# First batch of an attention-and-experts kernel: q and k of all four pairs of heads resident, row maxima one by one between tiles, the first pair's in two PSUM tiles

## Chip, cores and metric

The kernel runs on one core of a Trainium2 chip. The metric is device time in microseconds (us) of one execution. The engines are TensorE (PE, with its weight loads as PEld), VectorE (DVE), ScalarE (ACT), GpSimd (POOL) and SyncE (SP), which issues most DMAs. Each engine runs its own instructions in order and waits on semaphores for the others.

## Reference

```python
scores = matmul(q, k.transpose(0, 1, 3, 2)) / sqrt(64)      # q, k, v: (4 batches, 8 heads, 576, 64)
thresh = max(scores, axis=-1) - tau
scores = where(scores >= thresh, scores, -1e9)
attn   = exp(scores - max(scores)); attn /= attn.sum(-1) + 1e-9
x = (attn @ v).transpose(0, 2, 1, 3).reshape(2304, 512)
h = x @ w_in                                                  # first expert, 512 -> 2048 -> 512
x = ((a0 + a1*h + a2*h**2 + a3*h**3) / (1 + |b0|*|h| + |b1|*h**2 + 1e-6)) @ w_out
h = x @ w2_in                                                 # second expert, same sizes
y = where(h >= 1, h, where(h <= -1, 0, (h + 1)**2 / 4)) @ w2_out
```

The weights of both experts are stored as 64-bit floats; the kernel turns them into 16-bit pieces itself.

## The kernel before

The program has two stages. In the first, up to about 235 us, the attention of batch 0 runs alone (`first_attention`), while the sixteen weight halves of the first expert are loaded and converted beside it. In the second, the tokens go through the two experts in steps, a batch at a time; the attention of batches 1 to 3 and the sixteen halves of the second expert's weights (`w2`) are laid beside these steps.

Batch 0 is worked through in four pairs of heads, 0 to 3. For a pair, `prep_pair` loads q and k (tile `rqk`), scales and casts them on ScalarE (L203), takes the remainder on GpSimd (L207), transposes both by one DMA of 18 blocks of 128 x 128 into `qkT` (L339), and copies the two halves of k crosswise into `kT2` (L341, L342). Then `row_max` finds the row maxima. It makes eleven score tiles `sm` (eight of 512 columns, one of eight small pieces `t`, `r` and `rt`): two dots each on TensorE (L506, L507) and one reduction on VectorE (L510), all through one PSUM tile of tag `ph0`. The maxima are cut in three 16-bit pieces (`pcs`, L537, L539), turned into rows by small products `pmr` in the PSUM tile `aux` (L545; this tile also serves the products `pmmw`, `pg` and `pmmqke` of the weights and of the scales), and ScalarE copies them into `mrow` (L546). Only then can the nine tiles of the pair begin. A tile's transposed scores `st` are six products, of which every third subtracts the row maxima (L562 to L564); ScalarE takes the exponential (L566), VectorE applies the threshold (L567), and TensorE sums over v (L576). At the end of a pair ScalarE copies the sums out (L583, L584), and VectorE divides (L590 to L592) and writes the two 16-bit parts of the result `xT` (L597).

The weight halves go through VectorE in three passes (L223 to L225, `rw` to `wt`), ScalarE (L212, L241, L203) and GpSimd (L207).

`row_max` is a generator: in the tiles 0, 2 and 4 of a pair the program takes one step of the next pair's maxima, and after tile 5 it prepares the pair after that one.

```python
rows = row_max(pr + 1, *ahead[0][1:]) if ahead else iter(())
...
    if n % 9 in (0, 2, 4):
        mrow = next(rows, None)
    if n % 9 == 5 and pr + 2 < NP:
        ahead.append(prep_pair(0, pr + 2, False))
```

Written order is not yet the engines' order. Each of the `N_FIRST` steps of `first_attention` and each half of the weights gets a priority (`at(...)`), and a scheduler places every engine's instructions by priority and by its own estimate of when they are ready. The engines then run that order.

Of the kernel before, what the change touches and what calls it, by code (L numbers as in the profile page):

```python
# [9 lines left out]
F16 = mybir.dt.float16  # L10
# [29 lines left out]
def tile_attention_moe_moe2(  # L40
# [20 lines left out]
    P = 128  # L61
# [250 lines left out]
    def prep_pair(b, pr, on_vector=True):  # L312
# [39 lines left out]
    def scores(s, t, ab, qkT, kT2):  # L352
# [6 lines left out]
        k1 = qkT[:, C:, :].rearrange("p c s -> p (c s)")  # L359
        k2 = kT2.rearrange("p c s -> p (c s)")  # L360
        for rows, c, cols, keys in parts:
            at = 0
            for k0, n in keys:
                while n:
                    w = min(n, 512 - at % 512)
                    T.matmul(s[rows, at : at + w], qkT[:, c, cols], k1[:, k0 : k0 + w], start=True, stop=False)  # L366
                    T.matmul(s[rows, at : at + w], qkT[:, c, cols], k2[:, k0 : k0 + w], start=False, stop=True)  # L367
                    at, k0, n = at + w, k0 + w, n - w
# [127 lines left out]
    def row_max(pr, qkT, kT2):  # L496
        k1 = qkT[:, C:, :].rearrange("p c s -> p (c s)")
        k2 = kT2.rearrange("p c s -> p (c s)")
        mx = sp.tile([P, 18], F32, name=f"mx0_{pr}", tag="c2", bufs=3)

        def bank(name):
            return ps_1.tile([P, 512], F32, name=f"sm{pr}_{name}", tag="ph0")

        def dots(dst, c, cols, k0):
            n = dst.shape[-1]
            T.matmul(dst, qkT[:, c, cols], k1[:, k0 : k0 + n], start=True, stop=False)  # L506
            T.matmul(dst, qkT[:, c, cols], k2[:, k0 : k0 + n], start=False, stop=True)  # L507

        def most(n, src, m=1):
            V.tensor_reduce(mx[:, n : n + m], src, axis=AX.X, op=ALU.max)  # L510

        halves = [slice(i * ST, (i + 1) * ST) for i in range(2)]
        for ab in range(2):
# [4 lines left out]
            yield  # L518
# [12 lines left out]
        most(3 * NT + 1, s)  # L531
        n = 2 * NT + 1
# [7 lines left out]
        mrow = ap.tile([P, 2 * S], F16, name=f"mrow{pr}", tag="hl", bufs=N_ROW)  # L540
        G.memset(mrow, 0.0)
# [5 lines left out]
        yield mrow  # L547

    def transposed(pr, ab, t, data, n):

        con, qkT, kT2, mrow = data
# [3 lines left out]
        q1 = qkT[:, 0:C, :].rearrange("p c s -> p (c s)")  # L555
# [46 lines left out]
    def first_attention():  # L602

        ahead = [prep_pair(0, 0, False)]
        yield
        vv = first_v()
        yield
        xT[0] = [xp.tile([P, 2 * KT, TB], F16, name=f"xT0_{j}", tag="xT", bufs=NB) for j in range(NB)]
        ahead.append(prep_pair(0, 1, False))
        yield  # L610
        for mrow in row_max(0, *ahead[0][1:]):
            yield
        n = 0
        for pr in range(NP):
            con, qkT, kT2 = ahead.pop(0)
            data = con, qkT, kT2, mrow
            rows = row_max(pr + 1, *ahead[0][1:]) if ahead else iter(())
# [3 lines left out]
            for ab, t in [(0, t) for t in range(NT + 1)] + [(1, t) for t in range(NT)]:  # L621
# [24 lines left out]
    N_FIRST = 7 + 9 * NP  # L646
# [288 lines left out]
```

## Time and profile before

| what | us |
|---|---|
| three runs | 1308.18, 1313.86, 1312.43 (median 1312.43) |
| profiled execution | 1311.16, of which its span 1309.2 |
| TensorE busy | 1096.2 (84% of the span) |
| VectorE busy | 1022.1 (78%) |
| ScalarE busy | 823.1 (63%) |
| GpSimd busy | 504.7 (39%) |
| granted TensorE clock, mean over the span | 0.929 of full speed |

Busy time is time in which an engine executes; the span runs from the first instruction to the last. The stages of a program can have different limits, so the shares of the whole span are the first thing to look at and not the last.

### The profile page before, as it was taken

The page shows a single profiled execution, that of the slowest core. Times are in us where ns is not written, and L with a number is a line of the kernel's source. Part 1 is how long each engine was busy: PE and PEld are TensorE (multiplying, and loading weights), DVE is VectorE, ACT ScalarE, POOL GpSimd, SP SyncE. Part 2 cuts the span into 40 slices and gives each one's busy share as a digit, 9 for nine tenths or more (in the row PEclk, how much of TensorE's full clock was granted, in tenths as well). Part 3 has the DMA queues.
Part 4 walks back from the last instruction along what each step waited for, and adds up shares of the span by engine and source line. Part 5 has one row for each costly group of instructions (what it writes and reads, how often), then busy time and mean ns, then how long its engine had stood idle before and what let it go on. Part 6 is the DMA issues. An engine that isn't in the chain of part 4 may idle for free.

```text
span 1309.2 us, 31145 instructions
## 1 busy us (share of the span) xinstructions
PE 1096.2 (84%) x12354; PEld 977.9 (75%) x12354; DVE 1022.1 (78%) x2403; ACT 823.1 (63%) x1477; POOL 504.7 (39%) x678
## 2 busy tenths in 40 slices
PE   2686667678862799989988999999798999999998
PEld 1253334577751688889878899898688988999997
DVE  6676566989987987768999776799997767897431
ACT  3466446677745667767677577677775767676332
POOL 3123214444543564542146455421473554122221
PEclk9997768798985799989989999999999999999999
DMA  7625333533477765692359664911685559105100
GB/s 204 197 97 162 121 129 133 200 119 105 150 262 217 167 126 109 122 222 86 87 134 226 127 114 101 258 62 46 174 202 112 103 100 267 46 2 210 50 14 26
DMA packets 220274, 176.35 MB, mean 135 GB/s; under 512 B 181984, under 2 KB 193248, under 8 KB 211936
## 3 DMA queue, kind: packets, MB, share of 16 engines
q1 hardware_dynamic: 220128, 174.36, 50.0%
q8 instruction: 97, 1.59, 0.5%
q14 instruction: 49, 0.40, 0.1%
HBM read 106.83 MB, written 21.50 MB: 98 GB/s over the span
## 4 chain that ended last, share of the span: by engine, by line
PE 36%; DVE 15%; DMA 10%; issue 3%; POOL 3%; ACT 2%; SPq 1%; DVEq 0%; ACTq 0%; POOLq 0%
PE acc L834 15%; PE ph L820 15%; DMA eT<-hl 6%; PE pv L400 2%; DVE e L374 2%; POOL hl L385 2%; DMA qkT<-qk 2%; DVE sc L412 1%; DVE t L713 1%; DVE t L712 1%; PE s L367 1%; PE s L366 1%; DVE qk L210 1%; DMA rqk<-in_k_dram 1%; DVE t L714 1%
## 5 line engine op out<-in xcount | busy, mean ns | idle before, releaser
L834 PE MATMUL acc<-gg,wc 128*128 128x192 f16 x4608 | 431.9, 248 | 26.0 <-POOL gg L207 16.7
L820 PEld LDWEIGHTS <-wc 128*128 128x128 f16 x4608 | 393.4, 100 | 30.0 <-DVE t L709 20.2
L834 PEld LDWEIGHTS <-wc 128*128 128x128 f16 x4608 | 386.0, 99 | 29.1 <-issue 27.3
L207 POOL TENSOR_TENSOR gg<-t,gg 128x384 f16<-128x384 f32 x192 | 192.3, 1003 | 413.8 <-ACT gg L203 353.5
L820 PE MATMUL ph<-xT,wc 128*128 128x192 f16 x2304 | 221.4, 254 | 19.1 <-DVE t L709 15.1
L820 PE MATMUL ph<-yT,wc 128*128 128x192 f16 x2304 | 218.8, 249 | 1.6 <-DVE t L709 1.1
L385 POOL TENSOR_TENSOR hl<-e,hl 128x256 f16<-128x256 f32 x216 | 155.8, 741 | 0.0
L203 ACT CAST gg<-t 128x384 f16<-128x384 f32 x192 | 97.2, 508 | 69.4 <-DVE t L767 36.5
L374 DVE SCALAR_TENSOR_TENSOR e<-sc,nt,e 128x576 f32<-128x576 f32 x108 | 95.7, 886 | 32.3 <-ACT e L373 31.6
L766 DVE SCALAR_TENSOR_TENSOR t<-t,c 128x384 f32<-128x384 f32 x96 | 63.8, 664 | 69.9 <-ACT t L765 69.8
L383 POOL TENSOR_TENSOR hl<-e,hl 128x64 f16<-128x64 f32 x108 | 40.6, 376 | 165.2 <-ACT hl L382 162.4
L373 ACT ACTIVATE e<-sc,nt,con 128x576 f32<-128x576 f32 x108 | 93.5, 866 | 8.7 <-POOL hl L385 1.4
L382 ACT CAST hl<-e 128x576 f16<-128x576 f32 x108 | 72.3, 669 | 41.0 <-DVE e L374 39.0
L705 ACT ACTIVATE t<-ph,sc 128x384 f32<-128x384 f32 x96 | 55.4, 577 | 63.0 <-PE ph L820 62.9
L400 PE MATMUL pv<-v,eT 128*128 128x65 f16 (+3 forms) x1680 | 71.7, 196 | 25.3 <-DMA eT<-hl 25.2
L412 DVE TENSOR_SCALAR_CACHE_REDUCE sc<-s 128x576 f32<-128x576 f32 x108 | 80.8, 749 | 14.9 <-PE s L367 14.3
L765 ACT ACTIVATE t<-ph,c 128x384 f32<-128x384 f32 x96 | 63.8, 666 | 44.3 <-PE ph L820 43.7
L400 PEld LDWEIGHTS <-eT 128*128 128x128 f16 (+1 forms) x1680 | 64.3, 102 | 34.5 <-DMA eT<-hl 32.1
L207 POOL TENSOR_TENSOR wc<-wt,wc 128x256 f16<-128x256 f32 x64 | 47.7, 778 | 94.2 <-ACT wc L203 94.2
L710 ACT ACTIVATE t<-t,lc 128x384 f32<-128x384 f32 x96 | 67.9, 708 | 23.4 <-DVE t L707 22.9
L366 PE MATMUL s<-qkT 128*128 128x512 f16 (+1 forms) x240 | 65.0, 294 | 15.9 <-DVE sc L412 11.2
L712 DVE SCALAR_TENSOR_TENSOR t<-t,ka,t 128x384 f32<-128x384 f32 x96 | 65.8, 686 | 14.7 <-ACT t L711 14.0
(216 smaller groups left out, 1857.4 us busy)
## 6 DMA issues: line engine op xcount, KB each, us to landing
wc<-scratch SPq DMA_DIRECT2D x56, 1024.0 KB, 5.7
rw<-in_moe_w_in_dram SPq DMA_DIRECT2D x16, 1024.0 KB, 5.4
rw<-in_moe_w_out_dram SPq DMA_DIRECT2D x16, 1024.0 KB, 5.0
scratch<-wc SPq DMA_DIRECT2D x8, 1024.0 KB, 3.8
scratch<-wh SPq DMA_DIRECT2D x16, 512.0 KB, 3.0
kT<-qkT SPq DMA_DIRECT2D x32, 144.0 KB, 2.4
rqk<-in_q_dram SPq DMA_DIRECT2D x16, 256.0 KB, 3.1
rqk<-in_k_dram SPq DMA_DIRECT2D x16, 256.0 KB, 3.0
```

The costliest lines, as they stand in the source:

```text
L203: A.copy(hi, src)
L207: G.tensor_tensor(lo[:, p], src[:, p], hi[:, p], op=ALU.subtract)
L366: T.matmul(s[rows, at : at + w], qkT[:, c, cols], k1[:, k0 : k0 + w], start=True, stop=False)
L373: A.activation(e, s, AF.Exp, bias=nb, scale=con[:, 0:1])
L374: V.scalar_tensor_tensor(e, s, th, e, op0=ALU.is_ge, op1=ALU.mult)
L382: A.copy(hi, e)
L385: G.tensor_tensor(lo_w[:, p], e[:, whole][:, p], hi[:, whole][:, p], op=ALU.subtract)
L400: T.matmul(pv[rows, 0:w], eT[:, c, cols], vv[:, h * NT + x if x < NT else H * NT + h, at : at + w], start=(n == 0), stop=(n == len(blocks) ...
L412: V.tensor_scalar(s, banks[:, 0:S], 1.0, -LARGEST, op0=ALU.mult, op1=ALU.max, accum_out=mx)
L712: V.scalar_tensor_tensor(s, s, ka[:, 0:1], r, op0=ALU.add, op1=ALU.mult)
L820: last = T.matmul(ph[:, f, :], w[:, wx, kt, f * P : (f + 1) * P], rhs, start=(n == 0), stop=(n == 3 * KT - 1))
L834: T.matmul(dst, w[:, wx, f, d * P : (d + 1) * P], gg[:, gx, f, :], start=(i == 0 and f == 0 and n == 0 and d % 2 == 0), stop=(i == NCH - 1 ...
```

## The change

Pairs 2 and 3 get buffers of their own for q and k: three tiles each (`qT`, `kT`, `kT2`), in buffers of tags `eT` and `hl` that only the later batches used. They are filled by two transposes of nine blocks in place of one of eighteen. So all four pairs are prepared ahead of the first tile in written order. The two `mrow` tiles are fixed and cleared once. `row_max` gives way after each of its tiles (eleven steps in place of three); in each of a pair's first four tiles the program takes two steps of the next pair's maxima, in the others one. The first pair's maxima use two PSUM tiles (`acc` and `s`) in turn. `N_FIRST`, over which the priorities are spread, goes from 43 to 53.

```diff
-        qkT = ap.tile([P, 2 * C, P], F16, name=f"qkT{b}_{pr}", tag="qkT")
-        Q.dma_start_transpose(out=qkT, in_=qk.rearrange("p x c d -> p (x c d)"))
-        kT2 = ap.tile([P, C, P], F16, name=f"kT2{b}_{pr}", tag="kT2")
-        Q.dma_start(kT2[0:D], qkT[D : 2 * D, C : 2 * C, :])
-        Q.dma_start(kT2[D : 2 * D], qkT[0:D, C : 2 * C, :])
-        return con, qkT, kT2
+        if b > 0 or pr < 2:
+            qkT = ap.tile([P, 2 * C, P], F16, name=f"qkT{b}_{pr}", tag="qkT")
+            Q.dma_start_transpose(out=qkT, in_=qk.rearrange("p x c d -> p (x c d)"))
+            qT, kT = qkT[:, 0:C], qkT[:, C : 2 * C]
+            kT2 = ap.tile([P, C, P], F16, name=f"kT2{b}_{pr}", tag="kT2")
+        else:
+            qT, kT, kT2 = (ap.tile([P, C, P], F16, name=f"{x}{b}_{pr}", tag="eT" if pr == 2 else "hl", bufs=N_ROW)
+                           for x in ("qT", "kT", "kT2"))
+            for x, t in enumerate((qT, kT)):
+                Q.dma_start_transpose(out=t, in_=qk[:, x].rearrange("p c d -> p (c d)"))
+        Q.dma_start(kT2[0:D], kT[D : 2 * D])
+        Q.dma_start(kT2[D : 2 * D], kT[0:D])
+        return con, qT, kT, kT2
...
-    def row_max(pr, qkT, kT2):
+    def row_max(pr, qT, kT, kT2, mrow):
...
+        count = [0]
...
         def bank(name):
-            return ps_1.tile([P, 512], F32, name=f"sm{pr}_{name}", tag="ph0")
+            if pr > 0:
+                return ps_1.tile([P, 512], F32, name=f"sm{pr}_{name}", tag="ph0")
+            count[0] += 1
+            return ps_2.tile([P, 1024], F32, name=f"sm{pr}_{name}", tag="acc" if count[0] % 2 else "s")[:, 0:512]
...
-            yield
+                yield
...
-        mrow = ap.tile([P, 2 * S], F16, name=f"mrow{pr}", tag="hl", bufs=N_ROW)
-        G.memset(mrow, 0.0)
...
-        yield mrow
+        yield
...
-        ahead = [prep_pair(0, 0, False)]
+        pairs = [prep_pair(0, 0, False)]
...
+        mrows = [xp.tile([P, 1152], F16, name="mrow0", tag="yT", bufs=NB), mp.tile([P, 1152], F16, name="mrow1", tag="yo", bufs=1)]
+        for t in mrows:
+            G.memset(t, 0.0)
         yield
-        ahead.append(prep_pair(0, 1, False))
+        pairs.append(prep_pair(0, 1, False))
         yield
-        for mrow in row_max(0, *ahead[0][1:]):
+        for _ in row_max(0, *pairs[0][1:], mrows[0]):
+            yield
+        for pr in range(2, NP):
+            pairs.append(prep_pair(0, pr, False))
             yield
...
-                if n % 9 in (0, 2, 4):
-                    mrow = next(rows, None)
-                if n % 9 == 5 and pr + 2 < NP:
-                    ahead.append(prep_pair(0, pr + 2, False))
+                for _ in range(2 if n % 9 < 4 else 1):
+                    next(rows, None)
...
-    N_FIRST = 7 + 9 * NP
+    N_FIRST = 17 + 9 * NP
```

The change moves instructions on three engines. In the names below, `sm2_13` is a score tile of pair 2's maxima, `et1_0_0` the exponentials of pair 1's first tile, `st1_0_0` its scores, and the last number of a name is the buffer's serial number. Lines of the changed program lie 7 to 14 further down: the reduction is L521, the threshold L578, the passes over weights stay L223 to L225.

On VectorE, pair 2's maxima stand before the change between pair 1's last tile and pair 2's first:

```order
L510 TENSOR_REDUCE mx0_2_802<-sm2_13_887 128x1
L510 TENSOR_REDUCE mx0_2_802<-sm2_t_944 128x4 x2
L510 TENSOR_REDUCE mx0_2_802<-sm2_r_963 128x1
L510 TENSOR_REDUCE mx0_2_802<-sm2_rt_969 128x1
L534 TENSOR_TENSOR mx0_2_802<-mx0_2_802 128x9
L537 TENSOR_SCALAR pcs2_976<-mx0_2_802 128x9
L539 SCALAR_TENSOR_TENSOR mx0_2_802<-pcs2_976,mx0_2_802 128x9
...
L537 TENSOR_SCALAR pcs2_976<-mx0_2_802 128x9
L567 SCALAR_TENSOR_TENSOR et2_0_0_1153<-st2_0_0_1146,con0_2_691,et2_0_0_1153 128x576
```

With the change they stand between pair 0's result and pair 1's first tile:

```order
L608 SCALAR_TENSOR_TENSOR xT0_2_260<-x0_0_576,v0_s_254,xT0_2_260 128x192
L521 TENSOR_REDUCE mx0_2_898<-sm2_00_899 128x1
L521 TENSOR_REDUCE mx0_2_898<-sm2_01_903 128x1
...
L521 TENSOR_REDUCE mx0_2_898<-sm2_r_1077 128x1
L224 SCALAR_TENSOR_TENSOR wt0_4_0_929<-rw0_4_0_927,wt0_4_0_929 128x1024
L521 TENSOR_REDUCE mx0_2_898<-sm2_rt_1083 128x1
L225 SCALAR_TENSOR_TENSOR wt0_4_0_929<-rw0_4_0_927,wt0_4_0_929 128x1024
L223 TENSOR_SCALAR wt0_4_1_1038<-rw0_4_1_1036 128x1024
L547 TENSOR_TENSOR mx0_2_898<-mx0_2_898 128x9
L521 TENSOR_REDUCE mx0_3_1215<-sm3_00_1216 128x1
L578 SCALAR_TENSOR_TENSOR et1_0_0_893<-st1_0_0_886,con0_1_286,et1_0_0_893 128x576
```

The whole block of eleven moved up by one pair; pair 3's maxima (`sm3`), which stood behind pair 2's tiles, follow among pair 1's tiles.

On TensorE, the products that turn pair 1's maxima into rows (`pmr1`) stand before the change right behind the first products of pair 1's first tile, in the last tiles of pair 0:

```order
L576 MATMUL pv1_0_1_669<-et0_1_2_728,v32_222 128x288
L562 MATMUL st1_0_0_790<-qkT0_1_293 128x288
L563 MATMUL st1_0_0_790<-qkT0_1_293,kT20_1_295 128x288
L545 LDWEIGHTS pcs1_597
L545 MATMUL pmr1_0_605<-fixed_90,pcs1_597 3x128
...
L545 MATMUL pmr1_4_611<-fixed_90,pcs1_597 3x128
...
L564 MATMUL st1_0_0_790<-mrow1_603,fixed_90 128x288
```

With the change, ten of pair 2's eleven score tiles come in front of them:

```order
L573 MATMUL st1_0_1_907<-qkT0_1_297 128x288
L574 MATMUL st1_0_1_907<-qkT0_1_297,kT20_1_299 128x288
L517 MATMUL sm2_00_899<-kT0_2_531,qT0_2_530 128x512
L518 MATMUL sm2_00_899<-kT20_2_532,qT0_2_530 128x512
...
L517 MATMUL sm2_r_1077<-kT0_2_531,qT0_2_530 64x512
...
L556 MATMUL pmr1_0_802<-fixed_90,pcs1_796 3x128
...
L556 MATMUL pmr1_4_808<-fixed_90,pcs1_796 3x128
...
L575 MATMUL st1_0_0_886<-mrow1_262,fixed_90 128x288
```

So pair 1's row products moved behind pair 2's maxima, and with them the end of pair 1's first scores.

On SyncE's queue, a transpose of pair 1 stood behind two loads of weights, and pair 2's was one DMA:

```order
L236 DMA rw0_2_0_620<-in_moe_w_in_dram 128x4x512
L236 DMA rw0_2_1_733<-in_moe_w_out_dram 128x2x1024
L339 DMA_TRANSPOSE qkT0_1_293<-qk0_1_269 128x18x128
L316 DMA rqk0_2_670<-in_q_dram 128x2x256
...
L236 DMA rw0_4_1_1175<-in_moe_w_out_dram 128x2x1024
L339 DMA_TRANSPOSE qkT0_2_702<-qk0_2_678 128x18x128
L316 DMA rqk0_3_1017<-in_q_dram 128x2x256
L319 DMA rqk0_3_1017<-in_q_dram 64x64
L341 DMA kT20_2_704<-qkT0_2_702 64x1152
L342 DMA kT20_2_704<-qkT0_2_702 64x1152
```

With the change one of the two loads stands behind pair 1's transpose, and pair 2's transposes are two:

```order
L236 DMA rw0_1_1_386<-in_moe_w_out_dram 128x2x1024
L236 DMA rw0_2_0_466<-in_moe_w_in_dram 128x4x512
L340 DMA_TRANSPOSE qkT0_1_297<-qk0_1_273 128x18x128
L316 DMA rqk0_2_498<-in_q_dram 128x2x256
...
L236 DMA rw0_4_1_1036<-in_moe_w_out_dram 128x2x1024
L347 DMA_TRANSPOSE qT0_2_530<-qk0_2_506 128x9x128
L347 DMA_TRANSPOSE kT0_2_531<-qk0_2_506 128x9x128
L316 DMA rqk0_3_537<-in_q_dram 128x2x256
L319 DMA rqk0_3_537<-in_q_dram 64x64
L348 DMA kT20_2_532<-kT0_2_531 64x1152
L349 DMA kT20_2_532<-kT0_2_531 64x1152
```

Pair 2's transposes keep their place behind the weight loads up to `rw0_4_1`.

## Rows read from the trace of the kernel before

**Rows 1.** Busy time, share of the span and instructions of each engine
```profile
PE 1096.2 (84%) x12354; PEld 977.9 (75%) x12354; DVE 1022.1 (78%) x2403; ACT 823.1 (63%) x1477; POOL 504.7 (39%) x678
```

**Rows 2.** Windows cut at ScalarE's first and last exponentials of each pair
```profile
core 0: us, PE busy (x) PEld busy (x) DVE busy (x) ACT busy (x) POOL busy (x), PEclk, DMA share, GB/s
59.87:80.42 20.55, 19.83 (x125) 12.30 (x124) 15.74 (x32) 13.33 (x22) 4.11 (x7) 1.00 0.19 70
80.42:88.02 7.60, 4.94 (x29) 2.85 (x29) 5.55 (x8) 4.49 (x12) 1.98 (x3) 1.00 0.43 160
88.02:111.80 23.78, 19.70 (x102) 13.12 (x102) 16.12 (x38) 18.21 (x31) 4.19 (x6) 0.93 0.23 82
111.80:147.02 35.22, 18.69 (x77) 7.90 (x76) 22.75 (x39) 13.48 (x27) 11.20 (x13) 0.53 0.60 191
147.02:168.53 21.51, 18.52 (x104) 12.50 (x104) 14.64 (x33) 13.59 (x22) 5.08 (x6) 0.98 0.39 100
168.53:194.21 25.68, 14.86 (x83) 7.95 (x81) 16.82 (x32) 11.84 (x22) 5.72 (x9) 0.63 0.40 139
194.21:214.81 20.60, 18.50 (x98) 12.41 (x97) 14.51 (x29) 14.45 (x23) 6.64 (x8) 0.88 0.28 103
214.81:236.09 21.28, 10.88 (x56) 8.61 (x57) 15.18 (x49) 14.99 (x27) 6.67 (x9) 0.61 0.55 196
236.09:262.00 25.91, 15.89 (x140) 14.76 (x139) 25.01 (x45) 15.32 (x26) 16.10 (x14) 0.79 0.51 180
```

**Rows 3.** VectorE's timeline, pair 2's maxima: start, duration, line, operation, [idle <-releaser]
```profile
130.29 0.69 DVE L510 TENSOR_REDUCE mx<-sm 128x1 f32<-128x512 f32 x1 [1.10 <-PE sm L507]
132.09 0.69 DVE L510 TENSOR_REDUCE mx<-sm 128x1 f32<-128x512 f32 x1 [1.10 <-PE sm L507]
```

**Rows 4.** The same timeline, pair 3's maxima
```profile
173.50 0.69 DVE L510 TENSOR_REDUCE mx<-sm 128x1 f32<-128x512 f32 x1 [0.68 <-PE sm L507]
174.87 0.69 DVE L510 TENSOR_REDUCE mx<-sm 128x1 f32<-128x512 f32 x1 [0.68 <-PE sm L507]
```

**Rows 5.** Timelines of VectorE and ScalarE, last piece to first exponential of pair 2
```profile
142.81 0.17 DVE L537 TENSOR_SCALAR pcs<-mx 128x9 f16<-128x9 f32 x1
147.02 1.37 ACT L566 ACTIVATE et<-st,con 128x576 f32<-128x576 f32 x2
```

**Rows 6.** Timelines of ScalarE and TensorE, pair 2's cast and first dot
```profile
109.72 1.23 ACT L203 CAST qk<-rqk 128x576 f16<-128x576 f32 x2
120.02 0.61 PE L507 MATMUL sm<-kT,qkT 128*128 128x512 f16 x1 [0.52 <-DMA kT<-qkT]
```

**Rows 7.** View of tile eT, and DMA list (median us, issue to landing)
```profile
L387 SPq DMA_TRANSPOSE eT<-hl x108: 1242/1298/4039, 430.0 to 1105.0; - x108
...
eT<-hl SPq DMA_TRANSPOSE x108, 3.5
...
qkT<-qk SPq DMA_TRANSPOSE x16, 4.0
```

**Rows 8.** Timelines of SyncE's queue and TensorE, pair 1's transpose and first dot
```profile
41.30 5.62 SPq L339 DMA_TRANSPOSE qkT<-qk  x1
52.00 0.59 PE L506 MATMUL sm<-qkT 128*128 128x512 f16 x1 [0.32 <-DVE mx L510]
```

**Rows 9.** Groups by line and shape, 0 to 300 us (busy, mean ns)
```profile
L224 DVE SCALAR_TENSOR_TENSOR wt<-rw,wt 128x1024 int32<-128x1024 int32 x23 | 29.5, 1282 | 0.2
...
L223 DVE TENSOR_SCALAR wt<-rw 128x1024 int32<-128x1024 int32 x24 | 18.9, 786 | 6.8 <-POOL wc L207 3.3 <-DMA rw<-in_moe_w_out_dram 3.1 <-DMA rw<-in_moe_w_in_dram 0.3
...
L597 DVE SCALAR_TENSOR_TENSOR xT<-x,v_s,xT 128x192 f16<-128x192 f32 x12 | 5.4, 486 | 1.2 <-ACT xT L596 1.2
...
L591 DVE SCALAR_TENSOR_TENSOR d<-d,rd 128x576 f32<-128x576 f32 x4 | 3.0, 748 | 0.0
```

**Rows 10.** TensorE's timeline, first expert's first product
```profile
232.44 3.68 PE L820 MATMUL ph<-xT,wc 128*128 128x192 f16 x22 [0.54 <-DVE xT L597]
```

**Rows 11.** Windows of the time behind, and the chain's first long piece
```profile
262.00:393.00 131.00, 100.08 (x1052) 94.76 (x1049) 117.04 (x210) 89.13 (x147) 63.41 (x62) 0.90 0.45 159
...
391.22 6.31 DMA rv<-in_v_dram
```

More of the change, by code (lines that the diff above doesn't have):

```diff
@@ L337, in prep_pair, with scores @@
             split(qk[:, x, :, 0:D], qk[:, x, :, D : 2 * D], raw[:, x], s[:, x : x + 1], on_vector)
[L338 to L343 removed]
+        if b > 0 or pr < 2:
[11 more added lines that the diff above has]
+        return con, qT, kT, kT2
     ROWS = [(t, ab) for t in range(NT) for ab in range(2)] + [(NT, 0)]
     M = NT * P
[L352 removed]
+    def scores(s, t, ab, qT, kT, kT2):
         if t < NT:
@@ L365, in scores @@
                     w = min(n, 512 - at % 512)
-                    T.matmul(s[rows, at : at + w], qkT[:, c, cols], k1[:, k0 : k0 + w], start=True, stop=False)
-                    T.matmul(s[rows, at : at + w], qkT[:, c, cols], k2[:, k0 : k0 + w], start=False, stop=True)
+                    T.matmul(s[rows, at : at + w], qT[:, c, cols], k1[:, k0 : k0 + w], start=True, stop=False)
+                    T.matmul(s[rows, at : at + w], qT[:, c, cols], k2[:, k0 : k0 + w], start=False, stop=True)
                     at, k0, n = at + w, k0 + w, n - w
@@ L408, in att_rows @@
             banks = ps_2.tile([P, 1024], F32, name=f"s{name}_{r}", tag="s")
-            scores(banks, t, ab, qkT, kT2)
+            scores(banks, t, ab, qT, kT, kT2)
             mx, nt = small(1, f"mx{name}_{r}"), small(2, f"nt{name}_{r}")
@@ L546, in row_max @@
             A.copy(mrow[0:3, c0 * P : c1 * P], pm[0:3, 0 : (c1 - c0) * P])
-        yield mrow
+        yield
     def transposed(pr, ab, t, data, n):
-        con, qkT, kT2, mrow = data
+        con, qT, kT, kT2, mrow = data
         name = f"{pr}_{ab}_{t}"
@@ L561, in transposed @@
                 dst, of = s[r, z], slice(i * S + z * S // 2, i * S + (z + 1) * S // 2)
-                T.matmul(dst, qkT[:, C + c, cols], q1[:, of], start=True, stop=False)
+                T.matmul(dst, kT[:, c, cols], q1[:, of], start=True, stop=False)
                 T.matmul(dst, kT2[:, c, cols], q1[:, of], start=False, stop=False)
@@ L602, in first_attention @@
     def first_attention():
-        ahead = [prep_pair(0, 0, False)]
+        pairs = [prep_pair(0, 0, False)]
         yield
         vv = first_v()
+        xT[0] = [xp.tile([P, 2 * KT, TB], F16, name=f"xT0_{j}", tag="xT", bufs=NB) for j in range(NB)]
+        mrows = [xp.tile([P, 1152], F16, name="mrow0", tag="yT", bufs=NB), mp.tile([P, 1152], F16, name="mrow1", tag="yo", bufs=1)]
+        for t in mrows:
+            G.memset(t, 0.0)
         yield
-        xT[0] = [xp.tile([P, 2 * KT, TB], F16, name=f"xT0_{j}", tag="xT", bufs=NB) for j in range(NB)]
-        ahead.append(prep_pair(0, 1, False))
+        pairs.append(prep_pair(0, 1, False))
         yield
-        for mrow in row_max(0, *ahead[0][1:]):
+        for _ in row_max(0, *pairs[0][1:], mrows[0]):
+            yield
+        for pr in range(2, NP):
+            pairs.append(prep_pair(0, pr, False))
             yield
@@ L614, in first_attention @@
         for pr in range(NP):
-            con, qkT, kT2 = ahead.pop(0)
-            data = con, qkT, kT2, mrow
-            rows = row_max(pr + 1, *ahead[0][1:]) if ahead else iter(())
+            data = *pairs[pr], mrows[pr % 2]
+            rows = row_max(pr + 1, *pairs[pr + 1][1:], mrows[(pr + 1) % 2]) if pr + 1 < NP else iter(())
             x = ap.tile([P, S], F32, name=f"x0_{pr}", tag="e", bufs=N_SC)
```

12 lines of the change are left out of this document (6 added, 6 removed).

## Prediction, on record before the run

> **What bounds the kernel now.** I read the busy shares first: TensorE 84%, VectorE 78% of the span [rows 1]. No engine is full, so the shares don't say what the change is worth; it touches only the first stage, and this was cut into windows at ScalarE's first and last exponentials of each pair [rows 2]. The four pairs take 20.55, 23.78, 21.51 and 20.60 us, and between them lie stretches of 7.60, 35.22 and 25.68 us. In the two long ones TensorE's granted clock falls to 0.53 and 0.63 of full speed, nearer its lower level (1.2 GHz) than its upper (2.4), with TensorE busy 18.69 of 35.22 us. Nothing is full there: the stage waits on a chain. Inside it, the timeline of pair 2's maxima shows a reduction of 0.69 us every 1.80 us, idle 1.10 before each until TensorE's dots come [rows 3]: the one PSUM tile makes dots and reduction take turns. At the higher clock the pitch is 1.37 [rows 4]. From the last piece to the first exponential pass another 4.21 us [rows 5], and from pair 2's cast to its first second-half dot 10.3 [rows 6]. So a long stretch is preparation, eleven turns and row products, one after the other. The chain that ended last is of no help here; its first long piece starts at 391.22 [rows 11].
>
> **The change, stretch by stretch.** The sum runs from the first exponential (59.87) to the first expert's first product (232.44) [rows 2, 10].
>
> *Start of pair 0, 59.87 to 58.4.* Two tiles let dots and reductions overlap, so pair 0's maxima end earlier. But on TensorE their row products stand behind the first score tiles of pair 1, in both orders. In before the first such dot ran at 52.00, and the transpose that feeds it took 5.62 us to issue from 41.30, against a median landing of 4.0 [rows 7, 8]. With the change this transpose goes ahead of one load of weights. The least gain is none or a loss of about 1 (one more pitch of pair 1's maxima now stands ahead of the row products); the most is the 5.62 cut to a common length plus the finished maxima, a start near 51. I take 1.5 us.
>
> *Pair 0, 20.55 to 24.4.* VectorE gets one L223, one L224 and two L225 more (0.79 + 3 x 1.28, L225 being of L224's form) less one reduction of 0.69: 3.9 us [rows 3, 9]. TensorE is busy 19.83 of 20.55 here, so I count them in full; nothing, to all of it, are the bounds.
>
> *Pair 0 to pair 1, 7.60 to 36.* This is the new wait. Before, nothing of it was due here. Now ten of pair 2's eleven score tiles stand on TensorE ahead of pair 1's row products, and pair 2's cast comes on ScalarE behind pair 0's last exponential. From that exponential: itself and the scaling of q and k, three ScalarE instructions of a tile's size at 1.37 for two [rows 5], 2.1; cast to second-half dot 10.3 [rows 6]; and what the split transpose costs. A nine-block transpose issues in 1.3 and lands in 3.5, so the second lands 4.8 after the first began, where one of eighteen took 4.0: 0.8 more [rows 7]. That is 13.2. Then nine pitches of 1.80 to the tenth tile, since the clock of the like stretch was 0.53: 16.2 [rows 2, 3]; the tenth's own dots 1.3; pieces to exponential 4.2 [rows 5]; 1 for a weight product (`pg0_3_0`) between. Together 36. At the higher clock's 1.37 it would be 32; with a pass over weights in each reduction's place, as VectorE's order has at the end of the block, 41.
>
> The Trainium skill ("DMA: Bandwidth & Descriptors", section "Anatomy of one DMA") gives a DMA a fixed cost of about 2.0 us, mostly for the confirmed landing; it states this for DMAs that GpSimd issues. Were each second transpose to pay it in series, pairs 2 and 3 would pay about 4 us together by that figure, an estimate, where rows 7 make it 1.6 for both. The rows have durations for the same kind of transfer, and by them two on one queue overlap but for the issue.
>
> *Pair 1, 23.78 to 27.6.* Between its tiles come six reductions of pair 3 (4.1), five more passes over weights (0.79 + 4 x 1.28 = 5.9) and a reduction of 1152 columns, 1.3 by the 0.69 for 512, less pair 0's division, which is now done before (three of 0.75, three of 0.49: 3.7) [rows 3, 9]. Net 7.6. VectorE was busy 16.12 of 23.78 [rows 2], so there is room for all of it, but its instructions stand in order among thresholds that wait for exponentials. I take half; bounds nothing and 7.6.
>
> *Pair 1 to pair 2, 35.22 to 8; pair 2 to pair 3, 25.68 to 9.* The maxima are done by then. What is left is row products, copies and first scores, as between pairs 0 and 1 before: 7.60 [rows 2]. The second has three more weight instructions on ScalarE ahead of the copies. Bounds 7 and 13 each. These 44 us are the gain, of which the stretch ahead of pair 1 takes back 28.
>
> *Pairs 2 and 3, 21.51 to 23.1 and 20.60 to 21.6.* Pair 2 gets a set of three passes (3.35) and pair 1's division (3.7), and loses two reductions (1.4), the long one (1.3) and small ones (1.2): 3.1. Pair 3 gets two passes more (0.79 + 1.28 = 2.1) [rows 3, 9]. Half of each again.
>
> *Last exponential to the expert, 17.63 to 16* (214.81 to 232.44) [rows 2, 10]. The expert's constants, which stood on VectorE behind the division, now fill its wait ahead of it; bounds 15 and 18.
>
> Sum: 58.4 + 24.4 + 36 + 27.6 + 8 + 23.1 + 9 + 21.6 + 16 = 224.1 in place of 232.44, 8.3 us less.
>
> *Behind it.* VectorE now has two halves of w2 converted before the experts start, by its order: 2 x 3.35 = 6.7 us of passes [rows 9]. From 236.09 to 262 it is busy 25.01 of 25.91 [rows 2], and 117.04 of 131 after that [rows 11], so part of them comes back as time. I take 2.5; bounds nothing and 6. The two orders are the same again well before half of the program, and TensorE's work behind is unchanged, so I let the shift reach the end.
>
> Against the profiled execution (1311.16): 1311.16 - 8.3 - 2.5 = 1300.4. The median of the three runs is 1.3 above that profile, so 1302 for a median.
>
> **What it costs if the cover is gone.** Preparing pair 3 early (loads, cast, transposes) I cost at nothing: it runs under pair 2's twenty us of maxima. Were it late, pair 3's maxima would wait among pair 1's thresholds, and each of pair 1's later tiles with them. The queue then holds the weight loads behind the transposes on SyncE.
>
> **Rivals.**
> *A, no gain.* The block ahead of pair 1 takes 41 instead of 36, and pair 1 the whole 7.6 instead of half: 8.8 us back, about 1311. For it: TensorE cannot go round pair 2's maxima, and VectorE's order mixes conversions into them. Against it: in before the same block, with a division and six passes mixed in, still ended within 35.22.
>
> *B, slower.* One mechanism: VectorE can't take what is left after pair 1's start. Before, from pair 1's first exponential (88.02) to 236.09, it was busy 100.0 of 148.07 us, 0.68 [rows 2]. With the change, pair 2's reductions (7.5), pair 0's division (3.7), conversions (3.9) and small ones (3) lie ahead of that start, two w2 halves (6.7) come in: 88.6 are left. Pair 1 starts at 118.8 (58.4 + 24.4 + 36), so to be at the expert when before was, VectorE must be busy 88.6 of 117.3: 0.76. The best pair now has 15.74 of 20.55, 0.77; the others 0.68 to 0.70 [rows 2]. At 0.68 the stage ends 130 us after pair 1's start, at 249: 13 late, 1325. It decides at 0.76. Against it: the long stretches that held the share down are gone, and waits there were for the chain and not for VectorE's own order.
>
> *C, a larger gain.* Pair 1's k comes some 4 us sooner, since its transpose is no longer behind that load, and pair 0 starts at 53.5; the block ahead of pair 1 runs at the higher clock (36 to 32) and the passes moved forward give back 4.5. That is 4.9 + 4 + 2 = 11 more: 1291.
>
> **How the numbers follow.** Forecast 0.52, A 0.22, B 0.14, C 0.12. The likeliest's own range is 1295 to 1309 (the block's and pair 1's bounds, less than whole). A change under 0.5%, 6.5 us, can't be told from none. Faster by more (under 1305.9): nearly all of C and most of the forecast, 0.57. Within: A and the forecast's upper end, 0.27. Slower: B and a rest of A, 0.16. The range of 8 in 10 goes from 1287, inside which C lies, to 1318, which leaves out B and little else.
>
> **What would show it.** In the changed profile: pair 1's first exponential 30 us or more behind pair 0's last, with reductions of pair 2 about 1.8 us apart in between and the clock near 0.5 there; then two gaps under 13; VectorE busy 0.75 or more from pair 1's start to the expert; the first expert's product near 224. I would be wrong if pair 1 starts soon after pair 0 (the scores wait less for TensorE's order than I think), if the gaps of pairs 2 and 3 stay long (row products wait for the shared `aux` tile), or if the product comes at 224 and the end does not move (the stages behind have slack that takes the gain).

## The result

The changed kernel takes 1277.59 us (median of four runs, 1272.52 to 1280.61) against 1310.31 before, measured beside it: a ratio of 0.9745 with a 95% interval of 0.9699 to 0.9791. That is faster, as forecast, but three times the gain forecast (10.8 us by the prediction's sum, 32.7 between the medians), and below the range's low end. The profiled span is 1277.0 us, 32.2 less than before.

The page of the changed kernel, busy times against [rows 1]:

```profile
span 1277.0 us, 31136 instructions
PE 1078.5 (84%) x12354; PEld 967.6 (76%) x12354; DVE 1021.3 (80%) x2403; ACT 821.3 (64%) x1477; POOL 505.1 (40%) x676
```

VectorE does the same work in less time (80% of the span, 78% before). The windows, cut at the exponentials as in [rows 2], and last the whole stretch from pair 1's first exponential to the first expert:

```profile
core 0: us, PE busy (x) PEld busy (x) DVE busy (x) ACT busy (x) POOL busy (x), PEclk, DMA share, GB/s
57.21:77.50 20.29, 19.23 (x127) 12.51 (x125) 19.13 (x35) 13.35 (x21) 6.33 (x8) 1.00 0.58 203
77.50:110.73 33.23, 19.90 (x90) 9.45 (x89) 17.59 (x50) 18.21 (x34) 10.06 (x12) 0.61 0.51 149
110.73:134.58 23.85, 20.39 (x110) 12.56 (x109) 21.54 (x41) 14.46 (x22) 6.55 (x8) 0.98 0.46 153
134.58:143.32 8.74, 6.75 (x53) 4.29 (x53) 4.69 (x10) 7.64 (x15) 0.78 (x2) 0.96 0.54 194
143.32:167.34 24.02, 20.17 (x108) 13.06 (x107) 19.26 (x40) 16.98 (x27) 7.56 (x9) 0.87 0.38 131
167.34:175.15 7.81, 4.58 (x35) 2.71 (x33) 6.37 (x7) 6.01 (x15) 6.93 (x8) 1.00 0.40 149
175.15:199.95 24.80, 20.32 (x103) 13.51 (x103) 19.71 (x41) 16.65 (x30) 6.51 (x8) 0.86 0.49 173
199.95:218.29 18.34, 3.57 (x22) 2.51 (x21) 17.32 (x40) 11.03 (x20) 10.51 (x13) 0.70 0.57 219
110.73:218.29 107.56, 75.79 (x423) 48.64 (x422) 88.89 (x177) 72.77 (x124) 38.84 (x46) 0.88 0.47 167
```

The long stretches of 35.22 and 25.68 us are now 8.74 and 7.81; the short one of 7.60 ahead of pair 1 has become 33.23, at a granted clock of 0.61. The first expert's first product comes at 218.29, where it came at 232.44 [rows 10]: 14.2 us earlier. So 18 of the 32 us were gained behind the first stage. A ledger of VectorE shows where. Before, cut at the first expert's start, at its first and its last result for batch 0, and at the second expert's last result for batch 0:

```profile
core 0: us, PE busy (x) PEld busy (x) DVE busy (x) ACT busy (x) POOL busy (x), PEclk, DMA share, GB/s
0.00:232.40 232.40, 146.59 (x734) 84.61 (x735) 158.92 (x326) 122.14 (x209) 61.32 (x90) 0.84 0.49 151
232.40:301.60 69.20, 50.00 (x494) 47.21 (x493) 62.34 (x125) 50.53 (x83) 36.83 (x36) 0.87 0.41 145
301.60:389.10 87.50, 68.83 (x714) 65.19 (x714) 80.11 (x143) 56.39 (x93) 42.77 (x42) 0.89 0.50 175
389.10:594.10 205.00, 159.87 (x1990) 141.56 (x1991) 162.75 (x458) 132.51 (x245) 99.51 (x153) 0.86 0.70 165
594.10:1309.20 715.10, 670.95 (x8425) 639.31 (x8422) 557.94 (x1355) 461.52 (x850) 264.29 (x359) 0.99 0.47 115
```

and the changed kernel, cut at the same events:

```profile
0.00:218.30 218.30, 137.85 (x737) 81.93 (x738) 167.42 (x359) 128.81 (x218) 73.98 (x101) 0.85 0.56 180
218.30:280.30 62.00, 48.15 (x488) 45.66 (x488) 60.01 (x106) 45.33 (x77) 26.74 (x26) 0.87 0.38 136
280.30:368.00 87.70, 68.13 (x723) 63.80 (x720) 80.45 (x142) 59.26 (x97) 44.91 (x47) 0.94 0.52 180
368.00:562.70 194.70, 155.05 (x1985) 138.38 (x1986) 156.07 (x446) 126.22 (x239) 93.53 (x146) 0.91 0.71 158
562.70:1277.00 714.30, 669.31 (x8428) 637.78 (x8425) 557.38 (x1355) 461.65 (x850) 265.95 (x358) 0.99 0.47 115
```

VectorE's idle time is a window's length less its DVE column. Up to the first expert it falls from 73.5 to 50.9, in the next two windows from 14.3 to 9.2, in the fourth from 42.3 to 38.6: 31.2 in all, and the last window differs by 0.8. The changed kernel has 8.5 us more of VectorE work done when the first expert starts (167.42 against 158.92), and 8.7 less behind it: twenty of the thirty-two weight halves have had their last VectorE pass (L225) by then, eighteen before. The ledger says where the time went and not what made it go; the experiments ask that.

From the first expert's start to the second's last result for batch 0 as one window, and the part of it between the first expert's last result and the second's first, before:

```profile
232.40:594.10 361.70, 278.70 (x3198) 253.96 (x3198) 305.20 (x724) 239.43 (x420) 179.12 (x230) 0.87 0.60 164
389.10:494.70 105.60, 66.56 (x767) 56.34 (x768) 90.44 (x271) 64.22 (x117) 49.60 (x74) 0.75 0.69 169
```

and with the change:

```profile
218.30:562.70 344.40, 271.33 (x3193) 247.84 (x3193) 296.54 (x691) 230.81 (x412) 165.19 (x217) 0.91 0.60 160
368.00:456.60 88.60, 61.31 (x725) 52.99 (x726) 78.05 (x242) 56.19 (x105) 43.96 (x66) 0.83 0.67 160
```

The whole is 17.3 us shorter: 7.0 beside the first expert and 17.0 between the experts, of which 6.7 are given back behind the second's first result.

### The profile page after: what moved, and what is told of

Read it like the earlier page. It is cut to its first block, busy times and chain, and to the rows that moved or that the text cites. A ratio compares the mean times of both kernels' runs of the same rounds, so it can differ in the third digit from the quotient of the medians.

```text
span 1277.0 us, 31136 instructions
## 1 busy us (share of the span) xinstructions
PE 1078.5 (84%) x12354; PEld 967.6 (76%) x12354; DVE 1021.3 (80%) x2403; ACT 821.3 (64%) x1477; POOL 505.1 (40%) x676
## 4 chain that ended last, share of the span: by engine, by line
PE 38%; DVE 28%; DMA 12%; ACT 7%; issue 7%; POOL 6%; SPq 2%; DVEq 0%; ACTq 0%; POOLq 0%
PE acc L848 15%; PE ph L834 15%; DMA eT<-hl 7%; PE pv L407 2%; DVE t L727 2%; DMA qkT<-qk 2%; POOL hl L392 2%; DVE t L726 2%; DVE t L721 2%; DVE e L381 2%; DVE wt L224 2%; POOL wc L207 1%; DMA rqk<-in_k_dram 1%; DVE t L723 1%; ACT wt L212 1%
## 5 line engine op out<-in xcount | busy, mean ns | idle before, releaser
L834 PE MATMUL ph<-xT,wc 128*128 128x192 f16 x2304 | 216.1, 251 | 25.6 <-ACT xT L607 10.3
L419 DVE TENSOR_SCALAR_CACHE_REDUCE sc<-s 128x576 f32<-128x576 f32 x108 | 80.8, 748 | 13.0 <-PE s L374 12.7
L207 POOL TENSOR_TENSOR wc<-wt,wc 128x256 f16<-128x256 f32 x64 | 51.6, 838 | 82.9 <-ACT wc L203 82.8
L724 ACT ACTIVATE t<-t,lc 128x384 f32<-128x384 f32 x96 | 67.8, 707 | 17.0 <-DVE t L721 16.6
L726 DVE SCALAR_TENSOR_TENSOR t<-t,ka,t 128x384 f32<-128x384 f32 x96 | 64.0, 667 | 14.4 <-ACT t L725 14.2
```

The lines of the kernel that those rows point to most:

```text
L207: G.tensor_tensor(lo[:, p], src[:, p], hi[:, p], op=ALU.subtract)
L419: V.tensor_scalar(s, banks[:, 0:S], 1.0, -LARGEST, op0=ALU.mult, op1=ALU.max, accum_out=mx)
L724: A.activation(r, u, AF.Ln, bias=lc[:, 1:2], scale=lc[:, 0:1])
L726: V.scalar_tensor_tensor(s, s, ka[:, 0:1], r, op0=ALU.add, op1=ALU.mult)
L834: last = T.matmul(ph[:, f, :], w[:, wx, kt, f * P : (f + 1) * P], rhs, start=(n == 0), stop=(n == 3 * KT - 1))
```

## The experiments

All times are medians, with the ratio to the kernel before measured beside them; a lower ratio is faster. Windows and starts are read from one trace of each kernel.

**Halves back.** In the changed kernel the ten new steps move the weight halves forward, too. Here they count for nothing in the spread:

```diff
-        while halves and len(halves) * N_FIRST > 2 * NCH * (N_FIRST - 1 - n):
+        done = (n + 1) * 7 / 17 if n < 17 else n - 9
+        while halves and len(halves) * 43 > 2 * NCH * (43 - done):
```

> The changed kernel, with the weight halves spread over the steps of the first stage as before the change: the ten new steps count for nothing in the spread (the first 17 steps count as 7). By its order fewer halves come early, and the last half of w2 stands again behind the last result of the first expert's first batch. Theory W (the gain behind the first stage is the weight stream that runs 2 to 3 halves ahead, so that TensorE's hole between the first and the second expert, 51 us before and 32 after, shrinks): the experts start within 5 us of 218, the hole is back at 45 to 50, the time is 1288 to 1298. Rival F (the first stage alone carries the gain, the weights don't matter): 1274 to 1282.

Measured: 1271.35 us, 0.9682 (0.9644 to 0.9719). Theory W falls, and F's numbers are missed on the fast side. The first expert starts at 201.9, with eighteen halves through, as before. The stretch behind it up to the second expert's last result of batch 0, and the part between the experts:

```profile
201.90:549.80 347.90, 273.94 (x3195) 249.60 (x3195) 305.56 (x724) 240.14 (x420) 184.39 (x230) 0.90 0.63 170
362.10:452.90 90.80, 63.05 (x724) 53.45 (x724) 82.83 (x250) 59.25 (x108) 48.98 (x70) 0.83 0.69 156
```

Going back costs 3.5 us there (347.9 for 344.4) and gains 16 ahead of it. VectorE's work in the stretch is that of the kernel before again, 724 instructions and 305.6 us for 305.2, and yet the stretch is 13.8 us shorter than the 361.7 of before. So most of what the change gains behind the first stage comes without the passes that it moves forward. How sure the sizes are is shown by two kernels below that leave the first stage as it was (the stores' queue, and batch 1's attention one step later): they have 356.4 and 356.2 in this stretch. Against them the gain is 8 us, and the 3.5 can't be told from nothing.

**Halves ahead**, the opposite in the kernel before (`done = (n + 1) * 17 / 7 if n < 7 else n + 11`, of 53).

> The kernel before, with the weight halves spread as in the changed one (the first 7 steps count as 17). The pairs' work is as before. Theory W: the weight stream runs about one and a half halves ahead, the hole at the second expert shrinks by 5 to 10 us, the first stage is 0 to 5 us longer by the earlier passes: 1300 to 1308. Rival F: no gain without the pairs' change, the passes only crowd the first pairs: 1310 to 1320.

Measured: 1305.27, 0.9927 (0.9898 to 0.9956), inside W's numbers. But the execution profiled is the slowest of the five: its span is 1310.7 and its first expert starts at 233.5, so this gain isn't shown in the trace. Nor does the run test W there: ten halves are through at 100 us in place of seven, but at the first expert's start eighteen, as before.

**Preparation in the loop.** Own buffers, single steps and two tiles stay; pairs 2 and 3 are prepared behind tile 5 of an earlier pair.

```diff
-        for pr in range(2, NP):
-            pairs.append(prep_pair(0, pr, False))
-            yield
...
+                if n % 9 == 5 and pr + 2 < NP:
+                    pairs.append(prep_pair(0, pr + 2, False))
```

> The changed kernel with its own buffers for pairs 2 and 3 and its maxima one by one, but pairs 2 and 3 are prepared inside the loop, behind tile 5 of the pair two ahead, as before the change. Theory P (preparing all pairs up front is what lets a pair's maxima run beside another's tiles): two long stretches of 20 to 35 us between pairs are back, the experts start at 228 to 236, the time is 1292 to 1308. Rival M (the single steps of the maxima do it, wherever the preparation stands): the experts start at 215 to 222, 1274 to 1284.

Measured: 1281.95, 0.9758 (0.9726 to 0.979), the first expert at 213.8: theory P falls, and M's time holds. Of the long stretches between pairs one came back, 19.0 us ahead of pair 3.

**w2 late**: `WEIGHTS = (3, 23)` for `(0, 20)`.

> The changed kernel with w2's halves spread over the expert steps 3 to 23 in place of 0 to 20. By its order the last three halves then stand behind the start of batch 1's attention. If the hole between the experts is the wait of batch 1's v and q, k for the raw buffers and turns that the last w2 halves hold: the first scores of batch 1 come 5 to 15 us earlier than at 389, 1265 to 1275. If the second expert itself waits for the late halves: the hole stays at 30 us or grows, 1277 to 1292. Rival F: 1274 to 1282.

Measured: 1286.55, 0.9791 (0.9765 to 0.9818). VectorE takes batch 1's first scores (L419) 27 us earlier (362.0), and yet the kernel is no faster: 6 us slower by the ratios, with intervals that meet. As expected for a second expert that waits for the late halves, its next product comes at 414.67 (398.88 in the changed kernel), on TensorE behind the small products that scale the late halves, one of which waits 10.0 us for ScalarE's pass over its half (L241).

**More VectorE work**, early and late: `V.tensor_reduce(spin, gg, axis=AX.XYZ, op=ALU.max)` behind each first product of the steps of batch 0 (n = 0) or batch 2 (n = 4).

> The changed kernel with 24 reductions of a tile's expert values more on VectorE, one in each of the first expert's 24 steps for the first batch (768 values, about 0.9 us each, 20 us in all); they change no result. Theory V (up to about 560 us VectorE is the bound, so the change is worth the VectorE idle time that it removes by then): the time rises by 12 to 20 us, to 1289 to 1298. Rival G (the weights' chain or TensorE sets the end there, VectorE has room): it rises by 0 to 6, 1277 to 1284.

> The same 24 reductions in the first expert's 24 steps for the third batch, where TensorE is busy over 0.9 of the time. Theory V (VectorE is the bound only up to about 560 us): it rises by 0 to 6, 1277 to 1284. Rival G: no difference between early and late. If VectorE were the bound over the whole kernel: 12 to 20 here too.

Measured: 1291.6, 0.9841 (0.9779 to 0.9902) early, and 1298.7, 0.9875 (0.9836 to 0.9915) late. The 24 reductions take 0.94 us each, 22.5 in all. By the ratios they cost 13 early and 17 late, a difference that the intervals don't bear out. So added work on VectorE counts, but not only up to 560 us: that part of theory V falls. Early, the windows behind the first expert's start show why it isn't the whole:

```profile
216.70:383.40 166.70, 124.78 (x1214) 116.27 (x1213) 162.08 (x273) 108.77 (x177) 70.73 (x72) 0.88 0.44 153
383.40:567.10 183.70, 155.11 (x1984) 138.70 (x1985) 154.15 (x442) 124.22 (x234) 97.75 (x145) 0.93 0.72 161
567.10:1287.70 720.60, 673.57 (x8423) 641.02 (x8421) 559.13 (x1355) 461.79 (x850) 263.78 (x359) 0.99 0.47 114
```

The first is 17.0 us longer than the two of the changed kernel together (149.7), the second 11.0 shorter than its 194.7: most of the delay is taken up there. The third is 6.3 longer, though nothing was added to it, so that it stays open how much of the 10.7 us by which this span is longer the reductions caused.

**The parts alone and in pairs.** One tile in the changed kernel (`bank` gives the tag `ph0` to all pairs); two tiles in the kernel before; single steps in the kernel before (a `yield` behind every tile, two steps in tiles 0 to 3, one in the others); residence alone (the changed kernel with one tile and three steps); and the changed kernel with three steps:

```diff
-                for _ in range(2 if n % 9 < 4 else 1):
-                    next(rows, None)
+                if n % 9 in (0, 2, 4):
+                    next(rows, None)
```

> The changed kernel with pair 0's maxima through one PSUM tile as before. Theory V with the two tiles as one of its parts: pair 0's start and the first expert come 2 to 8 us later, 1280 to 1286. Rival: the row products of pair 0 stand behind pair 1's dots anyway, so the second tile brings nothing: 1274 to 1280.

> The kernel before with one part of the change, pair 0's maxima through two PSUM tiles. If the second tile's 11 us in the changed kernel (1288.6 without it) are pair 0's own shorter maxima: pair 0 starts earlier here too, 1298 to 1306. Rival (it gains only where the maxima of the next pair are single steps, since else pair 0's row products wait for pair 1's dots): 1307 to 1314.

> The kernel before with the maxima taken one by one (eleven steps, two a tile in a pair's first four tiles and one in the others), its buffers, the place of its preparation and its one PSUM tile left as they were. Theory M (the single steps bring most of the gain, also without residence): 1278 to 1290. Rival R (without buffers of their own pairs 2 and 3 come too late for their maxima to be spread, and the long stretches stay): 1298 to 1314.

> The kernel before with the third part of the change alone: own buffers for pairs 2 and 3, prepared up front, fixed tiles for the rows of maxima; the maxima in three steps and through one PSUM tile as before. If the parts add up (two tiles 9 to 11, single steps 22, together 31 to 33 of 33 to 34): 1304 to 1312. Rival (residence brings as much as the single steps, since either lets a pair's maxima run beside another's tiles): 1285 to 1298.

> The changed kernel with its maxima in three steps as before, own buffers and two PSUM tiles kept. If single steps add nothing to residence: 1272 to 1282. If the 11 us that the second tile brings need the single steps: 1284 to 1292.

| residence | single steps | two tiles | us | ratio (95%) |
|---|---|---|---|---|
| no | no | yes | 1301.61 | 0.9925 (0.990 to 0.995) |
| no | yes | no | 1289.07 | 0.9811 (0.9762 to 0.986) |
| yes | no | no | 1289.25 | 0.9819 (0.9793 to 0.9844) |
| yes | yes | no | 1288.6 | 0.9818 (0.9766 to 0.9869) |
| yes | no | yes | 1281.05 | 0.975 (0.9707 to 0.9794) |
| yes | yes | yes | 1277.59 | 0.9745 (0.9699 to 0.9791) |

Residence and single steps stand in for each other: either brings 1.8%, and the second adds nothing that can be told. The second tile brings 0.7% with or without them; alone it starts pair 0 at 49.6 in place of 59.9, but the first expert only 3.2 us earlier (229.2). The times that came true are M's for single steps, the rival's for residence, and the first one named for two tiles and for three steps; one tile took longer than either of its expectations. The second tile with single steps and the old buffers wasn't run. Residence and single steps reach the same by different ways. With residence alone, pair 0, the stretch ahead of pair 1, and all up to the first expert:

```profile
60.10:80.50 20.40, 19.72 (x127) 12.56 (x126) 15.22 (x32) 12.67 (x22) 3.26 (x5) 1.00 0.19 67
80.50:110.30 29.80, 19.25 (x89) 9.14 (x87) 18.15 (x46) 15.61 (x29) 9.37 (x12) 0.67 0.49 134
0.00:216.20 216.20, 141.58 (x734) 82.39 (x735) 155.95 (x327) 121.88 (x209) 61.56 (x88) 0.90 0.52 162
```

the block of pair 2's maxima stands ahead of pair 1 as in the changed kernel. With single steps alone that stretch is 5.7 us, the one ahead of pair 2 still 20.9, and all up to the first expert even less:

```profile
0.00:209.20 209.20, 135.75 (x737) 81.29 (x738) 160.91 (x336) 124.74 (x213) 66.00 (x94) 0.87 0.55 171
```

VectorE is idle for 60.3 and 48.3 us, for 73.5 before.

**Fewer passes at the stream's end**, in the kernel before: `as_float` leaves out L223 and L224 for the last three halves.

> The kernel before, in which the last three halves of w2 get one VectorE pass in place of three: the passes of L223 and L224 are left out for them, 6.2 us, which are as much as two halves' passes less behind the experts' start, and so these weights are not the reference's. The prediction valued that at 2.5 us. Theory W (the moved halves are worth more than their passes, since the stream's end lies in TensorE's hole between the experts): 10 to 16 us less, 1296 to 1302. Theory V (worth their VectorE time, no more): 3 to 7 less, 1305 to 1309. Rival: hidden, 1309 to 1314.

Measured: 1309.0, 0.9987 (0.9961 to 1.0012): hidden, or nearly. The 6.2 us of VectorE work left out bring 5 us at the most by the interval, and perhaps nothing; W falls, and V stands on the edge of its numbers.

**The stores' queue**, in the kernel before: `nc.scalar.dma_start` in L266.

> The kernel before with the stores of w2's halves (L266) issued from ScalarE in place of SyncE. In the chain of waits of before, the last store (423.39) stands on SyncE's queue ahead of the transposes that the first products behind the hole wait for (436.24). If that place is what holds the hole open: the first products of the second expert come 4 to 8 us earlier and the time is 1303 to 1309. Rival (another wait of the same length is beside it): 1309 to 1315, or more if ScalarE's order suffers.

Measured: 1307.46, 0.9995 (0.9973 to 1.0017): no difference.

**Batch 1's attention one step later**, in the kernel before: `ATTENTION = {1: (19, 50), ...` for `(18, 50)`. On TensorE's timeline, the last result's product (`my`) and the next of the second expert in before, and what stood ahead of it:

```profile
390.12 0.80 PE L182 MATMUL acc<-ident,my 128*128 128x128 f32 x2 [4.49 <-DVE my L779]
...
436.24 0.94 PE L400 MATMUL pv<-v,eT 128*128 128x65 f16 x14 [3.74 <-DMA eT<-hl]
436.99 3.23 PE L820 MATMUL ph<-yT,wc 128*128 128x192 f16 x19
```

and in the changed kernel:

```profile
369.00 0.49 PE L182 MATMUL acc<-ident,my 128*128 128x128 f32 x2 [1.88 <-DVE my L793]
...
398.88 1.44 PE L834 MATMUL ph<-yT,wc 128*128 128x192 f16 x8 [3.96 <-DVE t L781]
```

> The kernel before with the attention of batch 1 spread over the expert steps 19 to 50 in place of 18 to 50. By its order the first stage and the weights are the same as before, but on TensorE the second expert's third product now stands ahead of the first sums of batch 1's attention and of most of its first scores. Theory H (the 17 us behind the first stage come mostly from that order): the stretch from the first expert's last result to the next product of the second expert falls from 48 to about 30 us, and the time to 1298 to 1304. Rival (the gain behind comes with the earlier first stage and has nothing to do with this order): 1307 to 1313.

Measured: 1310.45, 0.9983 (0.9957 to 1.0009). The order did change, and the hole with it:

```profile
387.89 0.80 PE L182 MATMUL acc<-ident,my 128*128 128x128 f32 x2 [4.48 <-DVE my L779]
...
423.67 3.20 PE L820 MATMUL ph<-yT,wc 128*128 128x192 f16 x19 [1.41 <-DVE g L740]
```

The hole went from 46.9 to 35.8 us (29.9 in the changed kernel), and the second expert's last result came 7.7 us earlier (586.4 for 594.1), but from there to the end it took 721.6 us in place of 715.1. Theory H falls.

**Halves still later**, and the **two combinations** with a later attention of batch 1 (from step 20 in the changed kernel; from 19 with the halves back).

> The changed kernel with the weight halves still further back than in the run with halves back (1271.4): the first 17 steps count as 3 of 39. If early halves only crowd VectorE ahead of pair 0: pair 0 starts at 44 to 48 and the time is 1264 to 1271. If the weight stream then ends too late for the second expert: 1272 to 1285.

> The changed kernel with the weight halves back (1271.4) and the attention of batch 1 from step 19. If the two add: 1262 to 1269. If the order in the hole is right already: 1268 to 1275.

Measured: 1279.51, 0.9763 (0.9726 to 0.98) for the first: pair 0 starts at 48.2, but the first expert later (208.4) than with the halves back. 1269.4, 0.9675 (0.9645 to 0.9705) for the combination, which can't be told from halves back alone; it and that one are the fastest found that leave out nothing, about 0.7% under the changed kernel. The changed kernel with attention from step 20 took 1276.86, 0.9739: no difference.

**No maxima for pairs 2 and 3**, in the kernel before: `row_max` for `pr == 0` only, and the rows of pair 1 kept.

> The kernel before without the row maxima of pairs 2 and 3: their tiles subtract the rows of pair 1, so that their results are not the reference's. About 15 us of VectorE work and the two long stretches' turns go; the first expert should start 30 to 45 us earlier. Theory E (what comes back behind the first stage goes with an earlier start): from the first expert's start to the end 1055 to 1068 us, in place of 1077 before. Rival (it is an accident of the later order in the changed kernel): 1073 to 1080 there as before; and if the weight stream then becomes the bound, 1080 to 1095.

Measured: 1263.35, 0.9643 (0.9601 to 0.9685). The first expert starts at 189.3, 43 us earlier:

```profile
0.00:189.30 189.30, 123.03 (x629) 74.99 (x630) 134.93 (x272) 116.22 (x198) 58.14 (x83) 0.92 0.56 174
189.30:356.90 167.60, 120.43 (x1220) 111.69 (x1218) 154.86 (x293) 112.90 (x185) 82.18 (x84) 0.88 0.50 177
356.90:539.70 182.80, 152.52 (x1953) 135.80 (x1954) 158.61 (x440) 125.07 (x236) 102.66 (x151) 0.93 0.77 173
539.70:1257.60 717.90, 671.22 (x8460) 639.16 (x8457) 557.66 (x1364) 462.91 (x854) 263.54 (x360) 0.99 0.46 114
```

Behind it 1068.3 us, where before had 1076.8: 8.5 less, on the edge of theory E's numbers. VectorE has 8.3 us more work in the two middle windows than before and 19.6 less idle time.

## Why the prediction was wrong

**The stretch ahead of pair 1** was right in its mechanism and nearly in its size (36 forecast, 33.2). ScalarE's cast of pair 2 stands behind pair 0's last exponential (77.50), and the copies and the exponential behind it close the stretch:

```profile
79.46 1.23 ACT L203 CAST qk<-rqk 128x576 f16<-128x576 f32 x2
...
110.73 1.37 ACT L577 ACTIVATE et<-st,con 128x576 f32<-128x576 f32 x2
```

The two transposes on SyncE's queue, and the copy that waits for the second:

```profile
81.55 1.30 SPq L347 DMA_TRANSPOSE qT<-qk  x1
82.91 1.34 SPq L347 DMA_TRANSPOSE kT<-qk  x1
...
85.84 0.48 SPq L348 DMA_DIRECT2D kT<-kT  x1
```

From the first transpose to the copy pass 4.29 us. The first dots of pair 2 and its tenth tile on TensorE, with pair 1's row products right behind:

```profile
88.87 0.61 PE L518 MATMUL sm<-kT,qT 128*128 128x512 f16 x1 [2.33 <-DMA kT<-kT]
...
105.50 0.64 PE L517 MATMUL sm_r<-kT,qT 128*64 128x512 f16 x2
...
106.50 0.59 PE L556 MATMUL pmr<-fixed,pcs 128*3 128x128 f16 x4
```

and two of the reductions between:

```profile
99.31 0.69 DVE L521 TENSOR_REDUCE mx<-sm 128x1 f32<-128x512 f32 x1 [1.03 <-PE sm L518]
101.10 0.69 DVE L521 TENSOR_REDUCE mx<-sm 128x1 f32<-128x512 f32 x1 [1.10 <-PE sm L518]
```

From pair 0's last exponential to the second-half dot pass 11.4 us (13.2 forecast), from there to the tenth tile 16.6 (16.2), and from the row products to pair 1's first exponential 4.2 (4.2). The split cost 0.3 us over the 4.0 of one transpose of eighteen blocks [rows 7], where the prediction took 0.8. The Trainium skill ("DMA: Bandwidth & Descriptors", section "Anatomy of one DMA") gives a DMA that GpSimd issues a fixed cost of about 2.0 us; a second one in series would add that much, an estimate by this figure. The 0.3 on SyncE's queue doesn't agree with it.

**The gaps that were to vanish** did: 8.74 and 7.81 for 8 and 9. **The pairs** were mis-sized both ways: pair 0 20.3 for 24.4 and pair 1 23.9 for 27.6, where the extra passes cost nothing (VectorE's busy time rose from 15.74 to 19.13 and from 16.12 to 21.54 in windows as long as before), and pair 3 24.8 for 21.6; the tail 18.3 for 16. The sum, 218.3 for 224.1, was 5.8 us too slow.

**The step that failed** is "behind it", in its last sentence: "The two orders are the same again well before half of the program, and TensorE's work behind is unchanged, so I let the shift reach the end." It put every change in the waits behind the first stage at nothing. What was measured there is 17.3 us (361.7 to 344.4 between the first expert's start and the second's last result), where the prediction had 2.5 with bounds of nothing and 6, for the moved passes alone.

The ledger splits the 17.3 into 8.7 of VectorE work that had been done in the first stage (more than the 6.7 counted) and 8.6 of its idle time, 5.0 beside the first expert and 3.6 behind it. This is bookkeeping, and it would be wrong to read from it that the moved work came back in full: with the halves back none of that work is moved, and 13.8 of the 17.3 stay, as idle time of VectorE (42.3 us for 56.5; 8 to 14 us by the spread shown with that run). Two more kernels have eighteen halves through at the first expert's start: one tile and the preparation in the loop, with 302.6 and 310.2 us of VectorE work in the stretch, take 347.9 and 348.5 us for it. So the term for the passes was about right (3.5, if it can be told at all, for 2.5), and what failed is the part that had no term: the waits in that stretch, which grew shorter with the halves back too, most of all between the experts (105.6 to 90.8 us).

What makes these waits shorter isn't settled. It isn't the two halves that the changed kernel has through earlier, nor the passes of the last ones, nor the stores' queue, nor TensorE's order between the experts. A shorter first stage goes with it where this was made by other means (b_no_maxima), but single steps alone shortened the first stage by 23 us and kept 1080 us behind it. Whether the earlier start itself does it, or the order that the scheduler happens to lay between the experts, no run separates. And from the second expert's last result to the end the kernels differ by up to 7.3 us (714.3 to 721.6 in those quoted), for which no run has a cause.

**Rival B** fell: VectorE was to be busy 0.76 to keep up and was busy 88.89 of 107.56, 0.83. **Rival C** had the right direction by the wrong mechanism: the copy behind pair 1's transpose was issued 4.1 us sooner, as it said (44.82 for 48.92), but pair 0 started at 57.2 and not at 53.5, and the clock in the block was 0.61. **Rival A** fell: neither the block nor pair 1 was longer than forecast.

The prediction also took the change as one thing. By the table, its preparation up front and its single steps are two answers to one wait.

## What to carry to other kernels

Don't carry the gain of one stage unchanged to the end because the orders behind it are the same: here 14.2 us gained in the first stage became 32.2. Give the waits behind a changed stage a term of their own, with bounds, from the idle time that stands there (56.5 us of VectorE's here).

A ledger of the busiest engine, work and idle time by stage, shows where a gain lies. It doesn't show what the moved work is worth; set the work back, and see what stays (13.8 of 17.3 here, in one trace of each). And try the parts of a change alone before keeping all: two of three here did the same.

## What was not expected of the hardware

Two transposes of nine blocks, issued one behind the other (1.30 and 1.34 us), let the copy behind them start 4.29 us after the first issue; 22.5 us of extra VectorE reductions cost 13 us early, where VectorE was busy 140.46 of 149.7, and 17 late, by the ratios. And the same 724 VectorE instructions between the first expert's start and the second's last result of batch 0, 305 us of them, took 361.7 us in one kernel and 347.9 in another.
